# Two of three row blocks of the output projection by seven block products instead of eight, with the order of all operations in a table

## The chip, the cores and the metric

The kernel runs on one core of a Trainium2 chip. The core has a matrix engine (TensorE, PE in the profile, with its weight loads as PEld), a vector engine (VectorE, DVE), a scalar engine (ScalarE, ACT), a general engine (GpSimd, POOL) and a synchronisation engine (SyncE, SP), which here issues most DMA transfers. The metric is the device time of one execution in microseconds (us); less is better. All durations below come from the profile of one execution of the kernel before, the times from separate runs of it.

## What is computed

Attention over blocks of keys, followed by a gated feed-forward network. Cut to what matters:

```python
# q, k, v: 4 batches, 8 heads, 768 positions, 64 per head
ub = sum(maximum(q * k_min[chunk], q * k_max[chunk]))   # bound per query and chunk of 32 keys
sel = the 6 chunks of largest ub that are causal
attn = softmax(where(sel & causal, q @ k.T / 8, -1e9)) @ v
x = attn, heads side by side            # 3072 rows of 512
gate = sigmoid(x @ w_gate)              # 512 -> 1536
val  = x @ w_val                        # 512 -> 1536
out  = (gate * val) @ w_out             # 1536 -> 512, float32
```

The change touches the last line only: the output projection, a product of (3072 x 1536) by (1536 x 512).

## The kernel before, in words

The 24 row blocks of 128 positions (4 batches of 6) are gathered into eight units, u0 to u7, of three row blocks (384 rows) each. For every unit but u0 (which holds three first blocks with an attention of their own, the operations with an f in their names) the work is:

- Preparation: keys and queries are loaded, turned, and put into 16-bit operands (`kT`, `kt`, `hk`, `qf`, `qm`, `hq`); the bounds (`ub`, L1007) and the choice of chunks (`ubn`, `mx`, `ap`, `apt`, `hqm`) follow on DVE. Units u1 and u2 load keys and queries in rows and turn them on PE (`kn`, `kT`, `qn`, `qT`, L906); later units load whole batches (`k_1` to `k_3`, `q_1` to `q_3`) and turn them on DVE.
- Attention (`attend`): scores `sc` on PE (L1068), `exp` on ACT (L1079), the causal mask `cm` on POOL (L1085), the product with v, `pv`, on PE (L1101), the division `rz` and `x` on DVE, and a transpose `xps` on PE (L1128) with its copy `xT`.
- Feed-forward (`ffn`): for each of the 12 blocks of 128 hidden columns, `g` and `v` (each four matmuls of 128x384, L1151), `tanh` on ACT (L1159) and `hg` = (tanh + 1) * v on DVE (L1163). Then for each of the three row blocks (`tb` = 0, 1, 2) the output projection: 12 matmuls of 128x512 in three operations `o0`, `o1`, `o2` of four (L1176), the eviction `osb` with the factor 0.5 on ACT or DVE (L1185, L1186), and the store `out` of 128 rows of 2 KB by SP (L1187). In u7 the last row block goes in two parts, 384 and 128 columns (`o`, `ob`).

The weights `wg`, `wv`, `wo` come in three pieces each by DMA from POOL's queue (L723, L724, L729), converted to 16 bits on the way; POOL issues them between its other operations. The inputs are loaded through SP's queue in its order, the stores too.

The order of the work is set before the program is emitted. The functions above only add operations to a `Plan`, each with the engines that may run it and an estimated cost. `Plan.order` then places them: it walks time forward with those costs, and takes at each step the ready operation with the best priority; the priorities carry small offsets from a table (`NUDGES`), and landing times of DMAs come from another (`LANDS`). So every engine has one fixed list, and runs it in order. Buffers are numbered slots of a few kinds; PSUM is the kind `ps` with eight slots (banks), `big` is two large slots that hold the raw keys and queries of a batch one after the other, `hg` has 18 slots.

The operations that the prediction follows are, by their names before `_u`: `o0`, `o1`, `o2`, `osb`, `out` (these change), `g`, `v`, `hg`, `kT`, `qT`, `kn` (these keep their work and change place), and the DMA issues.

## Time and profile before

| | us |
|---|---|
| device time, median of 3 runs | 295.19 (294.67 to 295.32) |
| span of the profiled execution, first to last instruction | 293.1 |
| PE busy | 278.2 (95%) |
| ACT busy | 195.6 (67%) |
| DVE busy | 188.6 (64%) |
| POOL busy | 91.6 (31%) |
| granted TensorE clock, mean | 0.999 |

The profiled execution's own device time is not listed apart from the three runs. Its span is 293.1 us, and the median of the runs lies 2.1 us above the span; that part is start and end of the execution outside the program's own instructions.

How to read it: PE's busy time is that of its matmuls, whose ends are modelled and which overlap, so the duration of one matmul (379 ns for 128x512) is not what it costs in a row of matmuls. What it costs is the distance from one start to the next, which the chain and the timeline show: a line of either gives a start, a length and a number of instructions.

### The profile page before, as it was taken

How to read it: one execution, taken by the hardware profiler on the slowest of the kernel's cores; microseconds unless marked ns; L12 is line 12 of the kernel's file. 1: busy time of each engine (PE TensorE's matmuls, PEld its weight loads, DVE VectorE, ACT ScalarE, POOL GpSimd, SP SyncE). 2: the span in 40 equal slices, each digit the busy share in tenths (PEclk: the TensorE clock that was granted, in tenths of full speed). 3: DMA queues.
4: the chain of work that ended last, by engine and by line, in shares of the span. 5: the costliest groups of instructions: out<-in, count | busy, mean ns of one | idle time of the engine just before them, and what ended most of it. 6: DMA issues, size and time to landing. Idle time of an engine off the chain costs nothing.

```text
span 293.1 us, 6981 instructions
## 1 busy us (share of the span) xinstructions
PE 278.2 (95%) x2668; PEld 178.3 (61%) x2668; DVE 188.6 (64%) x560; ACT 195.6 (67%) x399; POOL 91.6 (31%) x162
## 2 busy tenths in 40 slices
PE   2849999999999999999999999999999999999995
PEld 2636655767674566556667667676566556655653
DVE  8366874997999289999999989654134114423320
ACT  7655847977984879458899998877463366332421
POOL 6744304834652337013326864212000010000000
PEclk9999999999999999999999999999999999999999
DMA  7999999989934999299992300001100020001002
GB/s 164 201 252 237 197 202 218 231 154 203 176 62 84 217 190 195 49 231 184 198 179 67 118 3 3 0 2 39 72 2 1 36 74 0 2 36 74 0 2 107
DMA packets 123377, 32.69 MB, mean 112 GB/s; under 512 B 111440, under 2 KB 120400, under 8 KB 123344
## 3 DMA queue, kind: packets, MB, share of 16 engines
q1 hardware_dynamic: 118592, 27.53, 44.5%
q0 software_dynamic: 4752, 4.72, 9.7%
q8 instruction: 21, 0.34, 0.5%
q14 instruction: 12, 0.10, 0.1%
HBM read 30.67 MB, written 6.29 MB: 126 GB/s over the span
## 4 chain that ended last, share of the span: by engine, by line
PE 76%; DMA 12%; DVE 6%; POOL 2%; SPq 1%; issue 1%; ACT 0%; DVEq 0%; ACTq 0%
PE o_u L1176 20%; PE v_u L1151 17%; PE g_u L1151 17%; PE sc_u L1068 10%; DMA wo<-in_moe_w_out_dram 8%; PE pv_u L1101 6%; DMA kq_u<-in_k_dram 3%; PE ube_u L1007 2%; PE xps_u L1128 2%; DMA vf<-in_v_dram 1%; SPq L747 1%; DVE kt L958 1%; DVE kx L792 1%; DVE kcr L792 1%; DVE qf_u L974 1%
## 5 line engine op out<-in xcount | busy, mean ns | idle before, releaser
L1079 ACT ACTIVATE att_u<-sc_u 128x512 f16<-128x512 f32 (+3 forms) x184 | 88.1, 551 | 14.4 <-PE sc_u L1068 13.6
L1163 DVE SCALAR_TENSOR_TENSOR hg_u<-gate_u,v_u 128x384 f16<-128x384 f16 x96 | 52.0, 546 | 54.1 <-PE v_u L1151 36.7
L1151 PE MATMUL g_u<-xT_u,wg 128*128 128x384 f16 x384 | 79.2, 329 | 0.0
L1151 PE MATMUL v_u<-xT_u,wv 128*128 128x384 f16 x384 | 78.8, 328 | 0.0
L1159 ACT ACTIVATE gate_u<-g_u 128x384 f16<-128x384 f32 x96 | 47.6, 496 | 38.4 <-DVE hg_u L1163 21.5
L1176 PE MATMUL o_u<-wo,hg_u 128*128 128x512 f16 (+1 forms) x288 | 67.4, 377 | 0.7 <-DMA wo<-in_moe_w_out_dram 0.7
L1085 POOL TENSOR_SCALAR_AFFINE_SELECT att_u<-att_u 128x384 f16<-128x384 f16 (+1 forms) x56 | 28.2, 509 | 109.7 <-ACT att_u L1079 108.9
L1151 PEld LDWEIGHTS <-wv 128*128 128x128 f16 x384 | 36.9, 98 | 22.9 <-issue 0.7
L1151 PEld LDWEIGHTS <-wg 128*128 128x128 f16 x384 | 36.5, 99 | 21.8 <-issue 1.5
L1176 PEld LDWEIGHTS <-hg_u 128*128 128x128 f16 x300 | 27.9, 98 | 27.8 <-issue 1.1
L1185 ACT ACTIVATE osb_u<-o_u 128x512 f32<-128x512 f32 (+1 forms) x20 | 12.0, 598 | 26.3 <-PE o_u L1176 24.6
L1101 PEld LDWEIGHTS <-att_u 128*128 128x128 f16 x640 | 25.5, 98 | 4.7
L1101 PE MATMUL pv_u<-v,att_u 128*128 128x65 f16 x640 | 27.9, 193 | 0.0
L1068 PE MATMUL sc_u<-hqo,hko 128*128 128x128 f16 (+2 forms) x220 | 27.8, 243 | 0.1
L1068 PE MATMUL sc_u<-hqe,hke 128*128 128x128 f16 (+2 forms) x220 | 27.2, 243 | 0.2 <-ACT att_u L1079 0.2
L1068 PEld LDWEIGHTS <-hke 128*128 128x128 f16 x220 | 16.8, 98 | 5.7 <-issue 1.2
L1068 PEld LDWEIGHTS <-hko 128*128 128x128 f16 x220 | 16.3, 98 | 4.8 <-issue 0.2
L784 POOL CAST v<-v 128x512 f16<-128x512 f32 x23 | 13.9, 616 | 13.5 <-DMA v<-in_v_dram 13.3
L581 DVE COPY xT_u<-xps_u 128x384 f16<-128x384 f16 (+1 forms) x17 | 5.8, 338 | 14.4 <-PE xps_u L1128 14.3
L1120 DVE TENSOR_TENSOR x_u<-pv_u,rz_u 128x384 f16<-128x384 f32 (+1 forms) x28 | 14.5, 524 | 0.4
L1030 DVE MAX8 mx_u<-ubn_u 128x8 f32<-128x8 f32 (+16 forms) x152 | 12.4, 158 | 0.1
L792 DVE TRANSPOSE_TENSOR_REDUCE kcr<-k 128x24 f32<-128x768 f32 x12 | 11.3, 945 | 0.0
(121 smaller groups left out, 308.4 us busy)
## 6 DMA issues: line engine op xcount, KB each, us to landing
v<-in_v_dram SPq DMA_DIRECT2D x23, 256.0 KB, 4.7
out_dram<-osb_u SPq DMA_DIRECT2D x23, 256.0 KB, 2.3
k<-in_k_dram SPq DMA_DIRECT2D x12, 384.0 KB, 4.8
q<-in_q_dram SPq DMA_DIRECT2D x12, 384.0 KB, 5.6
wg<-in_moe_w_gate_dram POOLq DMA_DIRECT2D x3, 512.0 KB, 9.0
wv<-in_moe_w_val_dram POOLq DMA_DIRECT2D x3, 512.0 KB, 10.9
wo<-in_moe_w_out_dram POOLq DMA_DIRECT2D x3, 512.0 KB, 21.4
kf<-in_k_dram SPq DMA_DIRECT2D x8, 128.0 KB, 3.1
```

Source lines behind the costliest of these rows:

```text
L784: plan.add(f"v16_{b}_{ib}", {POOL: pool(H * D)}, lambda e: nc.gpsimd.tensor_copy(v16[b % 2][:, ib, :, 0:D], at(t)), reads=[t], writes=[("v ...
L792: plan.add(f"kx{m}_{name}_{p}", {DVE: dve(size)}, lambda e, m=m, op=op: nc.vector.tensor_reduce(out=outs[m](), in_=src(), op=op, axis=AX.X ...
L1030: nc.vector.max(at(mx)[:, e_, j, :], at(ubn)[:, e_, j, 0:max(8, u.seen[j])])
L1068: nc.tensor.matmul(at(t)[:, o:o + 128 * m], hk[b % 2][e_][:, p, 128 * jb:128 * jb + 128], hq[u.side][e_][:, p, 128 * x:128 * (x + m)], sta ...
L1079: plan.add(f"exp_{u.name}_{h}_{y}", {ACT: act(n)}, lambda e, t=t, att=att, b0=b0, n=n: nc.scalar.activation(at(att)[:, b0:b0 + n], at(t), ...
L1085: nc.gpsimd.affine_select(out=dv, in_=dv, compare_op=ALU.is_ge, fill=0.0, base=0, pattern=[[0, u.m], [1, 128]], channel_multiplier=-1)
L1101: nc.tensor.matmul(at(pv)[:, last, x, :], at(att)[:, c:c + 128], v16[b % 2][:, jb, h, :], start=(jb == 0), stop=(jb == ib))
L1120: plan.add(f"x_{u.name}_{p}", {DVE: dve(u.t)}, lambda e: nc.vector.tensor_tensor(at(x_).rearrange("p a (e d) -> p e a d", e=2), at(pv)[:, ...
L1151: nc.tensor.matmul(at(t), w16[:, c, 128 * fb:128 * fb + 128], at(u.xt)[:, c, :], start=(c == 0), stop=(c == 3))
L1159: plan.add(f"tanh_{u.name}_{fb}", {ACT: act(T)}, lambda e, g=g, gate=gate: nc.scalar.activation(at(gate), at(g), AF.Tanh, scale=0.5), read ...
L1163: plan.add(f"hg_{u.name}_{fb}", {DVE: dve(T)}, lambda e, w_=w_, gate=gate, hg=hg: nc.vector.scalar_tensor_tensor(at(hg), at(gate), 1.0, at ...
L1176: nc.tensor.matmul(at(o), at(hgs[fc])[:, 128 * tb:128 * tb + 128], wo16[:, fc, lo:hi], start=(fc == 0), stop=(fc == NFB - 1))
```

## The change

For units u4 to u7, the row blocks 0 and 1 are no longer projected one after the other. The function `pair` treats the two row blocks together as a 2x2 block product: rows in two halves (row block 0, row block 1), the 1536 hidden columns in two halves (of every four column blocks the first two and the last two), and the 512 output columns in two halves of 256. By the scheme of Strassen and Winograd the product of two 2x2 block matrices needs seven block products instead of eight, and sums of blocks before and after:

- `weight_sums` makes four sums of blocks of `w_out` once (`tw0` to `tw3`, in three pieces j each, 12 operations of 128x512 16-bit numbers, DVE or POOL). They live in slot 0 of `big` behind the raw keys of batch 3.
- For each unit, `sw0` to `sw3` (three pieces each, 12 operations of 128x256 16-bit numbers, DVE or POOL) make the sums of hidden blocks. They and the 32-bit results live in slot 1 of `big`, behind the raw queries of batch 3.
- The seven products `p1` to `p7` are each six matmuls of 128x256 in two operations (four and two matmuls, the second with a z), into six PSUM banks; `p2` and `p6` share one.
- Six evictions `p1s`, `c11`, `u4`, `c12`, `c22`, `c21` (`c11` and `c22` are 512 wide, the others 256) add the products up in SBUF; all but `p1s` read SBUF and PSUM on DVE. `c11` takes `p2` and `p6` together.
- Then the two stores of 128 rows of 2 KB.

The third row block of each unit, and units u0 to u3, are projected as before. `hg` becomes nine slots of two column blocks each. The key "ffn", which kept the feed-forward products of all units in the order in which they were added, is gone. The planner (`walk`, `landings`, `settle`, the priorities) is gone too: `Plan.order` reads one table with every operation and its engine, and one with every buffer's slot.

```diff
-    def order(self):
-        nudge = {n: int(x) for n, x in (w.rsplit(":", 1) for w in NUDGES.split())}
...
-        out = self.walk({op: lands[op.name] for op in self.ops if op.dma is not None}, prio=prio)
-        out, _ = self.settle([(op, op.engine) for op in out])
+    def order(self):
+        ops = {op.name: op for op in self.ops}
...
+        for w in ORDER.split():
+            name, _, e = w.partition("=")
+            op = ops[name]
+            op.engine = {"P": PE, "A": ACT, "V": DVE, "G": POOL, "S": SP}[e]
...
+ORDER = """
+kf1_0=S kf0_0=S ident=G kfT_0=P kf16_0=A epat0=V epat=G hkp011=G hkp000=V hkp001=A hkp100=V hkp010=V ap1=V v10=G k2_u1=S kn_u1_2=V
+qf1_0=S kf0_1=S qf0_0=S qfT_0=P kT_u1_2=P kxf1=V ap0=V ident16=V kcr0=V qf16_0=A scf_0=P expf_0_1=A cmf_0_1=G qf1_1=S wg0=G
...
+xpsf_1_0=P expf_1_1=A cmf_1_1=G hkf1=G vf1_2=G wv0=G kx1_u1_0=V kt_u1_0=V expf_2_0=A cmf_2_0=G expf_2_1=A cmf_2_1=G hkf0=G wv1=G
...
+c12_u7=V c22_u7=V out_u7_0=S osbb_u7_2=A o0_u7_2=P o2_u6_2=P osb_u6_2=A out_u6_2=S outb_u7_2=S o1_u7_2=P o2_u7_2=P osb_u7_2=V
+out_u7_2=S p4_u7=P p4z_u7=P c21_u7=V out_u7_1=S
...
+    PAIRED = (4, 5, 6, 7)
+    tw = Buf("big", "tw", [128, 4, 3, 2, 256], F16)
+    sw = Buf("big", "sw", [128, 3072])
...
+            for n, (a, b) in enumerate(((12, 11), (22, 0), (22, 12), (21, 1))):
+                made.append(plan.add(f"tw{n}_{j}", {POOL: pool2(512), DVE: dve(512, 2)}, lambda e, n=n, a=a, b=b, w=w, out_=out_: both(e).tensor_tensor(
+                    out_(n), w[a](), w[b]() if b > 1 else out_(b), ALU.subtract),
...
+        def product(name, to, side, a, b, reads):
+            for part, js in (("", (0, 1)), ("z", (2,))):
+                def emit(e, js=js):
+                    for j in js:
+                        for i in range(2):
+                            nc.tensor.matmul(at(to)[:, side], a(j)[:, i], b(j)[:, i], start=j == i == 0, stop=j == 2 and i == 1)
...
+        product("p1", p1, 0, lambda j: block(j, 0, 0), w_(0, 0), h(0))
...
+        product("p2", p26, 0, lambda j: block(j, 0, 1), w_(1, 0), h(1))
+        product("p6", p26, 1, lambda j: sums(1, j), t_(1), st(1, 1))
+        onto("c11", p26, 2, slice(0, 3, 2), lambda: four()[:, 1:2].to_broadcast([128, 2, 256]), [key[1]])
+        product("p5", p5, 0, lambda j: sums(0, j), t_(0), st(0, 0))
+        onto("u4", p5, 1, slice(3, 4), lambda: four()[:, 2:3], [key[2]])
+        product("p3", p3, 0, lambda j: sums(3, j), w_(1, 1), lambda j: [(sw, j, 3)])
+        onto("c12", p3, 1, slice(1, 2), lambda: four()[:, 3:4], [key[3]])
+        store(u, 0, "", lambda: at(sw)[:, 1536:2048], rows[0], 0, 512, [key[0], key[1]], next_)
+        product("p7", p7, 0, lambda j: sums(2, j), t_(2), st(2, 2))
+        onto("c22", p7, 2, slice(2, 4), lambda: four()[:, 2:4], [key[2], key[3]])
+        product("p4", p4, 0, lambda j: block(j, 1, 1), t_(3), lambda j: h(1)(j) + [(tw, 3, j)])
+        onto("c21", p4, 1, slice(2, 3), lambda: four()[:, 2:3], [key[2]])
+        store(u, 1, "", lambda: at(sw)[:, 2048:2560], rows[1], 0, 512, [key[2], key[3]], next_)
...
-        for tb in range(3):
+        if u.i in PAIRED:
+            pair(u, hgs, [rows[0], rows[1]], next_)
+        for tb in range(2 if u.i in PAIRED else 0, 3):
```

In the table the letter behind a name is its engine (P for PE, A for ACT, V for DVE, G for POOL, S for SP), and each engine runs its entries in the order of the table. What it does differently from the list before, as far as the prediction speaks of it:

- On SP the first loads were `kf0_0 qf0_0 kf1_0 qf1_0 vf_0` and so on, with the eight loads of u1 behind the 15 of the first blocks. Now `kf1_0 kf0_0` come first, `k2_u1` third and `k0_u1` eleventh; `k3_u1` is the 22nd load in both.
- On PE, `kT_u1_3`, `qT_u1_0`, `qT_u1_1` and `qT_u1_2` stood behind `g_u0_0`; now they stand ahead of it. The scores of u1 stand ahead of `g_u0_8` to `g_u0_11`.
- On POOL, two operations lay between `wg0` and `wv0`; now eight lie between (`v16_0_0 cmf_0_0 cmf_1_0 vf1_1 vc_1 cmf_1_1 hkf1 vf1_2`, then `wv0`), and `wv1` comes ahead of `wg1`. The sums `tw` and `sw` go to POOL in 6 and 26 cases and to DVE in 6 and 22.
- Of the operations that both have, 40 move from DVE to ACT, 24 from ACT to DVE, 27 from ACT to POOL, 23 from DVE to POOL, 11 from POOL to ACT and 6 from POOL to DVE.
- At the end, PE's last entries were `o` and `ob` of the third row block of u7; now they are `o1_u7_2 o2_u7_2 p4_u7 p4z_u7`, with `osb_u7_2` and `c21_u7` on DVE and the stores `out_u7_2` and `out_u7_1`.

721 lines of the change are left out of this document (304 added, 417 removed), and 2 rows, old and new, of the table plan.

## The prediction, made before the result was known

> **What bounds the kernel now.** I read the page's busy times first, then busy time by stage, then PE's waits, then the chain.
>
> ```profile
> PE 278.2 (95%) x2668; PEld 178.3 (61%) x2668; DVE 188.6 (64%) x560; ACT 195.6 (67%) x399; POOL 91.6 (31%) x162
> ```
>
> ```profile
> core 0: us, PE busy (x) PEld busy (x) DVE busy (x) ACT busy (x) POOL busy (x), PEclk, DMA share, GB/s
> 0.00:23.20 23.20, 13.05 (x94) 9.87 (x95) 14.02 (x38) 15.09 (x25) 14.22 (x29) 1.00 0.98 212
> 23.20:50.00 26.80, 25.89 (x182) 14.99 (x181) 17.97 (x61) 17.63 (x41) 7.99 (x15) 1.00 1.18 210
> 50.00:90.00 40.00, 39.33 (x480) 27.38 (x477) 36.49 (x100) 34.74 (x78) 23.20 (x44) 1.00 0.91 169
> 90.00:290.00 200.00, 199.94 (x1924) 126.05 (x1916) 120.10 (x364) 127.87 (x259) 46.21 (x76) 1.00 0.35 76
> 290.00:293.10 3.10, 0.00 (x0) 0.00 (x0) 0.00 (x0) 0.26 (x1) 0.00 (x0) 0.94 0.24 85
> ```
>
> The stages carry the argument. From 90 to 290 us PE is busy for 199.94 of 200 us, while DVE, ACT and POOL are busy for 120, 128 and 46. In this stage lies all the work of units u4 to u7, so work taken off PE there shortens the kernel one for one, as long as its inputs still come in time. PE's idle time is 10.15 us before 23.2, 0.91 up to 50, 0.67 up to 90, and the 3.1 at the end.
>
> ```profile
> PE kfT L820 <- DMA kf<-in_k_dram: 5.7, 2, 5.0
> PE kT_u L906 <- ACT kn_u L579: 2.4, 1, 2.4
> ...
> PE o_u L1176 <- DMA wo<-in_moe_w_out_dram: 0.7, 1, 0.7
> ```
>
> PE's waits say the same: the first loads, then one wait of 2.4 us for u1's keys, and one of 0.7 us for the last piece of `wo`. Columns: total us, times, longest.
>
> **Term 1, the products.** In a row of matmuls a matmul costs the distance to the next start. The chain gives it for 512 columns, the timeline for 256:
>
> ```profile
> 91.21 5.18 PE o_u L1176 x24
> ```
>
> ```profile
> 143.21 0.38 PE L1068 MATMUL sc_u<-hqo,hko 128*128 128x256 f16 x2
> 143.43 0.38 PE L1068 MATMUL sc_u<-hqe,hke 128*128 128x256 f16 x2
> 143.65 0.65 PE L1151 MATMUL g_u<-xT_u,wg 128*128 128x384 f16 x3
> ```
>
> 24 matmuls of 512 in 5.18 us are 216 ns each, and they are exactly two row blocks. Four of 256 from 143.21 to 143.65 are 109 to 110 ns each (I take 109), each with a weight load of its own, as the new ones have. A unit now spends 24 x 216 = 5.18 us, and will spend 7 x 6 x 109 = 4.58 us. Four units: 4 x 0.606 = 2.42 us less. All of it is on PE's path: **-2.42**.
>
> Could 256 columns be too short to cover the weight load?
>
> ```profile
> L1176 PEld LDWEIGHTS <-hg_u 128*128 128x128 f16 x300 | 27.9, 98 | 27.8 <-issue 1.1
> ```
>
> A load lasts 98 ns, below 109, and the four rows of scores ran at 109 with loads between. The Trainium skill, page "TensorE: Matmul & The Clock Gate", section "Back-to-back issue gap", speaks against the change: it says that in a stream of pairs of load and matmul the spacing is set by both, about 81 ns at 128 columns and 131 at 512. An estimate from these two, 98 ns at 256, would make a unit dearer by 42 x 98 - 24 x 131 = 0.97 us, 3.9 us in all. The trace does not agree with its figure for 512: 216 ns, not 131. I go by the rows.
>
> **Term 2, the sums.** Per unit there are 12 `sw`, two of 512 and three of 256 columns among the results on DVE, and `p1s`; two `osb` go. Once there are 12 `tw`. Prices by the nearest rows:
>
> ```profile
> L1085 POOL TENSOR_SCALAR_AFFINE_SELECT att_u<-att_u 128x384 f16<-128x384 f16 x48 | 24.9, 526 | 100.9 <-ACT att_u L1079 100.3 <-PE sc_u L1068 0.3
> L784 POOL CAST v<-v 128x512 f16<-128x512 f32 x23 | 13.9, 616 | 13.5 <-DMA v<-in_v_dram 13.3
> ...
> L583 POOL COPY hqo<-apt_u 64x768 f16<-64x768 f16 x3 | 2.7, 892 | 5.5 <-DVE apt_u L1041 4.7 <-DVE rz_u L1118 0.8
> ...
> L799 POOL TENSOR_TENSOR kcr<-kx,kcr 128x96 f32<-128x96 f32 x2 | 0.8, 386 | 0.8 <-DVE rz_u L1118 0.8
> ...
> L799 POOL TENSOR_TENSOR kcr<-kx_u,kcr 128x48 f32<-128x48 f32 x1 | 0.3, 285 | 0.1
> ```
>
> ```profile
> L879 DVE TENSOR_TENSOR xf<-pvf,rzf 128x256 f16<-128x256 f32 x8 | 3.3, 420 | 0.1
> ...
> L1186 DVE TENSOR_SCALAR osb_u<-o_u 128x512 f32<-128x512 f32 x4 | 2.7, 676 | 4.2 <-PE o_u L1176 4.2
> ```
>
> On DVE a sum of 256 is at most 0.42 us, a result of 512 is 0.68, so the 22 + 6 sums and 20 results cost some 22 x 0.42 + 6 x 0.68 + 8 x 0.68 + 12 x 0.42 = 24 us of DVE, in a stretch of 200 us in which it now idles for 80. On POOL 48 more elements cost 0.10 us, 2.1 ns each, so 256 cost 0.72 us and 512 cost 1.26: 26 x 0.72 + 6 x 1.26 = 26 us, in a stretch in which it idles for 154. Neither becomes the bound. What can show is the queue behind one product. In u4, POOL must run between the last `hg` that `sw0_u4_1` reads and PE's `p6_u4`, by the table, `sw0_u4_0 tw1_1 sw1_u4_0`, a copy of 768, a cast, a mask, `tw1_2 sw0_u4_1 sw1_u4_1`: 2 x 1.26 + 4 x 0.72 + 0.89 + 0.62 + 0.53, some 7.4 us, while PE's entries from `v_u4_6` to `p6_u4` come to 9.5 us at the distances above. The second half, `p6z_u4`, is 0.4 us later and needs two more sums, 1.44 us, so its margin is about 1 us. Behind a late `p6` stands everything on PE. I take **+0.2** for such waits; ends 0 (the margins hold) and +1.5 (see rival C).
>
> **Term 3, the end.** PE's last work was 12 matmuls of 128 columns, then a copy and a 64 KB store.
>
> ```profile
> L1185 ACT ACTIVATE osb_u<-ob_u x1: 278/278/278, 290.0 to 290.0; 128x128 f32<-128x128 f32 x1
> ```
>
> ```profile
> out_dram<-osb_u SPq DMA_DIRECT2D x23, 256.0 KB, 2.3
> ...
> out_dram<-osb_u SPq DMA_DIRECT2D x1, 64.0 KB, 1.7
> ```
>
> Now `p4z_u7` is last, then `c21` on DVE (0.42 by the row of 256 above, for 0.28) and a store of 256 KB right behind one of 192 KB. That is 0.14 longer for the sum and 0 to 0.6 for the store; I take **+0.45**, ends +0.1 and +0.75. The other stores and sums of u7 lie under the 3.4 us of `o0_u7_2`, `o2_u6_2`, `o1_u7_2`, `o2_u7_2` and `p4` that PE has after `p7z`.
>
> **Term 4, the new order ahead of u4.** This is the unknown; it can be as large as term 1.
>
> ```profile
> 15.63 0.41 PE L886 MATMUL xpsf<-ident,xf 128*128 128x128 f16 x2
> 18.44 0.90 PE L906 MATMUL kT_u<-ident,kn_u 128*128 128x128 f32 x3 [2.40 <-ACT kn_u L579]
> ...
> 23.20 1.49 PE L1151 MATMUL g_u<-xT_u,wg 128*128 128x384 f16 x4
> 24.48 1.49 PE L1151 MATMUL v_u<-xT_u,wv 128*128 128x384 f16 x4
> ```
>
> ```profile
> 15.12 0.92 SPq L758 DMA_DIRECT2D kq_u<-in_k_dram  x1
> ```
>
> ```profile
> kq_u<-in_k_dram SPq DMA_DIRECT2D x4, 192.0 KB, 9.3
> ```
>
> `g_u0_0` starts at 23.20, and the first matmuls cost 0.32 us each (1.28 us for four), twice the 0.163 of later ones: PE comes out of its gaps slow, which costs about 10 x 0.16 = 1.6 us. In the new order `kT_u1_3` stands ahead of `g_u0_0`. Its load, `k3_u1`, is the 22nd on SP as before; it was issued at 15.12, and with 9.3 us to land (the median of the four) is there at 24.4. With 0.5 for its copy and 0.7 for its turn, `g_u0_0` starts at 25.6: 2.4 later, of which four transposes done earlier give back 4 x 0.33 = 1.3. So +1.1, unless PE is at full speed by then, since it turns u1's keys and queries without long gaps just before; that gives up to 1.6 back, -0.5. For the other side, the first product waits for two loads instead of three, and `k2_u1` and `k0_u1` come early enough to fill the gap of 2.4 us after 15.63: gains of up to 3 us if the whole opening moves up with them. From 50 to 90 us, where DVE is busy for 36.5 of 40 us, 63 entries leave DVE and 30 come to it: 0.67 us of PE's waits could go. I take **-0.3** for all of this, near the middle of the walk's -0.5 and +1.1 and a small gain behind it; ends -3 and +1.7.
>
> **The sum.** Span 293.1 - 2.42 + 0.2 + 0.45 - 0.3 = 291.03. The median of the runs lies 2.1 us above the span of the profiled execution, which I carry over: **293.1 us**, 0.7% below 295.19. Ends of the unknown terms around the forecast: 291.0 to 294.6.
>
> **The rivals.**
>
> B. The opening gains what the ends allow: term 4 at -3 gives 290.4. For it speaks that 10.15 us of PE's idle time lie before 23.2; against it that about 4 of these are the first landing, and that the late loads are the same bytes.
>
> C. The sums on POOL come late, in u4 and u5 (20 of the 26 `sw` there). The mechanism is seen in the opening: copies of one shape take longer when POOL and DVE run together.
>
> ```profile
> 4.13 1.51 DVE L581 COPY hko<-epat 64x1536 f16<-64x1536 f16 x3
> ...
> 5.66 1.91 DVE L581 COPY hke<-epat 64x1536 f16<-64x1536 f16 x3
> ...
> 7.10 0.93 POOL L583 COPY hke<-kf 64x512 f16<-64x512 f16 x1
> ```
>
> ```profile
> L583 POOL COPY hqo<-apt_u 64x512 f16<-64x512 f16 x1 | 0.6, 602 | 2.6 <-DVE apt_u L1041 2.6
> ```
>
> The second three DVE copies overlap POOL's copy at 7.10, and take 0.4 us longer; the POOL copy takes 0.93 against 0.60. The Trainium skill's page "SBUF — State Buffer", section "Who interferes with whom", has the rule: DVE and GpSimd share one port pair as a lock, also when a DVE instruction has two SBUF inputs, as the sums have. The rows agree with it. If each of some eight sums in front of a product slips by 0.35 us, that is 2.8 us against margins of 1 to 2: about 1 us in each of u4 and u5, 295.0 us.
>
> D. It ends slower: the weights come late. `wv0` stood two POOL operations behind `wg0`; now eight lie between, the last of which wait for `cmf_1_1` and so for the second block's exponentials.
>
> ```profile
> 9.96 0.93 POOL L723 DMA_DIRECT2D wg<-in_moe_w_gate_dram  x1
> ...
> 12.07 0.76 POOL L724 DMA_DIRECT2D wv<-in_moe_w_val_dram  x1
> ```
>
> ```profile
> wg<-in_moe_w_gate_dram POOLq DMA_DIRECT2D x3, 512.0 KB, 9.0
> ```
>
> ```profile
> 24.56 24.20 DMA wo<-in_moe_w_out_dram
> ```
>
> With the median of 9.0 us `wg0` was there at 19.0. If `wv0` is issued only then, POOL's DMA queue runs dry, and all seven pieces behind it slip by what it loses; the last piece of `wo` landed at 48.76 (24.56 + 24.20), and PE had to wait for it. At that time PE had done 28 us of work at the distances above, so it had lost 20.8; in the new order 33 us of work lie ahead of `o2_u0_0`, and PE comes to it at some 53. A slip below 4 us is covered; one of 7.5 us costs 3.3 us and gives 296.4. It decides from a slip of 6.9 us, where the time is 0.2% above before.
>
> E. The weight loads are not covered at 256 columns: 4 x 18 more loads of 98 ns, 7.1 us, 300 us. The rows at 143.21 speak against it.
>
> **How the numbers follow.** A difference of 0.2% (0.6 us) is about what a measurement of this kernel can tell from none. Forecast 0.53 (291.0 to 294.6, all faster); B 0.17 (faster); C 0.10 (0.08 within 0.2%, 0.02 just faster); D 0.18 and E 0.02 (slower). So faster 0.72, same 0.08, slower 0.20. The range reaches from just below B to D: 290.2 to 296.4.
>
> **What would show it.** Term 1: between starts, 109 ns in the `p` products, 42 of them per unit, and PE still busy for all but 0.3 us from 90 us on. Term 2: PE's waits name no POOL or DVE sum for more than 0.3 us in total, C is right if they do. Term 3: from PE's end to the end of the span 3.6 us, for 3.1. Term 4: the start of the first `g_u`, and PE's idle time before 50 us, 11.1 us now; D is right if PE waits for `wo` or `wv` there. The prediction is wrong above all if term 4 lies outside its ends.

## The result, and the profile after

The changed kernel takes 292.12 us (median of 4 runs, 291.77 to 292.85) against 294.93 us (median of 4 runs, 294.09 to 295.32): a ratio of 0.9913, 95% interval 0.9886 to 0.9939. It is faster, by 2.8 us. The profiled execution took 292.16 us and has a span of 290.5 us, 2.7 us less than before (290.46 for 293.12 in the traces).

The page's busy times of the changed kernel, then its busy time by stage (columns as before; the first stage ends at the start of the first `g_u`):

```profile
PE 275.3 (95%) x2740; PEld 185.4 (64%) x2740; DVE 201.3 (69%) x577; ACT 189.3 (65%) x393; POOL 145.6 (50%) x227
```

```profile
0.00:24.76 24.76, 15.15 (x106) 12.04 (x107) 14.68 (x34) 16.02 (x28) 16.70 (x31) 0.88 0.98 218
24.76:50.00 25.24, 25.19 (x239) 16.18 (x238) 16.35 (x58) 21.47 (x48) 14.46 (x26) 0.98 1.21 211
50.00:90.00 40.00, 40.00 (x433) 26.42 (x432) 35.35 (x104) 31.21 (x69) 25.92 (x46) 1.00 0.99 185
90.00:290.00 200.00, 194.93 (x1968) 130.73 (x1966) 134.89 (x383) 120.56 (x251) 88.49 (x126) 1.00 0.33 73
```

The number ahead of the DMA share is the granted TensorE clock. Here it is 0.50 from 19.0 to 24.76 us. The 1.00 in before's first rows can't be set against it: before's trace has no clock record ahead of 26.5 us, and its first products start 0.32 us apart too.

PE ends at 286.80 instead of 289.94, so 3.2 of the 5.07 us that the last stage is idle lie behind PE's end. PE's waits name two that before didn't have, on DVE's `x_u` and on POOL's mask:

```profile
PE sc_u L891 <- DVE x_u L943: 0.9, 1, 0.9
...
PE pv_u L924 <- POOL att_u L908: 0.8, 1, 0.8
```

**The products** run at the distance that the prediction took. In the timeline of PE, 12 matmuls start at 207.95 and the next at 209.26:

```profile
207.95 1.47 PE L1012 MATMUL p_u<-tw,sw 128*128 128x256 f16 x12
209.26 0.82 PE L1012 MATMUL p_u<-wo,sw 128*128 128x256 f16 x6
```

That is 1.31 us for 12, 109 ns each. No wait of PE names a sum of a product.

**A measure for the rest.** PE's busy time hides short waits, since the modelled ends of matmuls overlap the next start. So I counted for each matmul the distance that it costs in a row (0.417 ns a column and 2.6 ns, which gives 109 at 256 columns and 216 at 512; the 32-bit ones, 360 of 2668 before, by the median of their own distances), and took the sum of the matmuls begun before a time from that time. The difference is what PE has lost until then. All kernels of this section and the next, in us:

| lost until | 25 | 50 | 100 | 160 | 190 | 205 | PE's end |
|---|---|---|---|---|---|---|---|
| before | 14.7 | 18.0 | 20.5 | 23.1 | 25.7 | 25.7 | 25.9 |
| changed | 14.0 | 15.9 | 16.8 | 20.0 | 24.8 | 24.9 | 25.1 |
| products_only | 14.9 | 18.6 | 21.2 | 23.7 | 28.9 | 29.7 | 32.2 |
| products_spread | 13.6 | 18.0 | 20.5 | 23.1 | 25.7 | 29.5 | 30.2 |
| products_u5_u7 | 13.9 | 18.1 | 20.7 | 23.2 | 25.8 | 25.8 | 26.2 |
| order_only | 13.6 | 16.4 | 17.6 | 21.0 | 24.8 | 25.8 | 27.2 |
| order_only2 | 13.2 | 15.7 | 17.2 | 20.3 | 24.1 | 24.6 | 29.1 |
| before_opening | 13.8 | 28.3 | 30.8 | 35.2 | 38.9 | 40.1 | 40.6 |
| new_first35 | 14.1 | 22.4 | 25.4 | 28.0 | 30.6 | 30.6 | 30.8 |
| new_first90 | 14.0 | 16.2 | 18.9 | 21.5 | 24.0 | 24.1 | 24.3 |
| sums_later | 13.2 | 14.8 | 16.3 | 19.6 | 23.5 | 23.5 | 23.8 |
| mask_earlier | 13.9 | 16.2 | 17.6 | 20.7 | 25.5 | 25.6 | 25.9 |
| end_as_before | 13.0 | 14.5 | 15.6 | 18.8 | 23.7 | 23.8 | 24.3 |
| all_three | 14.0 | 16.0 | 17.7 | 20.8 | 24.5 | 24.7 | 25.2 |

PE's work by the same count is 264.03 us before and 261.66 with four paired units. The levels of the table are too high by a part that all rows share. The 288 small 32-bit products of the bounds (`ub`) run eight at a time: seven starts are 7 ns apart, and the next eight follow after 0.06 to 0.3 us. Their median of 7 ns counts most of their time as lost, some 6 us by the end, and about 1.9 us of what each kernel loses between 160 and 190 us. Differences between rows hardly suffer from it.

One kernel's opening differs from execution to execution: the changed kernel and its four relatives at the bottom run the same program there, and have lost 14.5 to 16.2 at 50 us. So a difference between two rows at one time means something from about 2 us, or where it arises inside one stretch. At 100 us these five have lost 15.6 to 17.7, and the four kernels with the order of before 20.5 to 21.2.

The first two rows hold the result. The new order is 3.7 us ahead at 100 us and 3.1 at 160; then it loses 4.8 up to 190 where before loses 2.6, and arrives 0.8 ahead. With 2.37 less work and an end that is 0.5 longer: -0.8 - 2.37 + 0.5 = -2.7, which is the difference of the spans.

**The two new waits.** The first, at 170 us. PE has two `pv_u` done and goes on 1.02 us later, where two take 0.06; POOL, whose mask it needs, ran an operation of 2.12 us (`qm_u7_0`, moved to POOL by the table; its sister took 0.85 on ACT) and, in its order, another mask and a copy ahead of that mask. Timeline of PE, then of POOL, then of ACT:

```profile
170.46 0.22 PE L924 MATMUL pv_u<-v,att_u 128*128 128x65 f16 x2
171.48 0.47 PE L924 MATMUL pv_u<-v,att_u 128*128 128x65 f16 x10 [0.79 <-POOL att_u L908]
```

```profile
167.34 2.12 POOL L631 TENSOR_SCALAR qm_u<-qf_u 128x768 f32<-128x768 f32 x1 [1.78 <-PE ubo_u L830]
169.43 0.52 POOL L908 TENSOR_SCALAR_AFFINE_SELECT att_u<-att_u 128x384 f16<-128x384 f16 x1
170.01 0.82 POOL L406 COPY hko<-kt 64x768 f16<-64x768 f16 x1
170.90 0.52 POOL L908 TENSOR_SCALAR_AFFINE_SELECT att_u<-att_u 128x384 f16<-128x384 f16 x1
```

```profile
167.17 0.85 ACT L629 ACTIVATE qm_u<-qf_u 128x768 f32<-128x768 f32 x1 [0.93 <-PE ubo_u L830]
```

The second, at 182 us. PE waits for the division `x_u6_1`; by the count above this costs 1.10 us. In front of the division DVE has three sums of the weights, which take 1.03, 0.76 and 0.82 us where others of the same shape take 0.41. Timeline of PE, of DVE, and of POOL beside it:

```profile
183.63 0.38 PE L891 MATMUL sc_u<-hqe,hke 128*128 128x128 f16 x4 [0.94 <-DVE x_u L943]
```

```profile
179.16 1.03 DVE L976 TENSOR_TENSOR tw<-wo 128x512 f16<-128x512 f16 x1
180.12 0.54 DVE L1086 SCALAR_TENSOR_TENSOR hg_u<-gate_u,v_u 128x384 f16<-128x384 f16 x1
180.59 0.76 DVE L976 TENSOR_TENSOR tw<-wo 128x512 f16<-128x512 f16 x1
181.26 0.82 DVE L976 TENSOR_TENSOR tw<-wo,tw 128x512 f16<-128x512 f16 x1
...
183.04 0.53 DVE L943 TENSOR_TENSOR x_u<-pv_u,rz_u 128x384 f16<-128x384 f32 x1
...
193.37 0.41 DVE L976 TENSOR_TENSOR tw<-wo 128x512 f16<-128x512 f16 x1
```

```profile
178.88 1.04 POOL L406 CAST hqe<-qf_u 64x768 f16<-64x768 f32 x1
180.55 0.52 POOL L908 TENSOR_SCALAR_AFFINE_SELECT att_u<-att_u 128x384 f16<-128x384 f16 x1 [0.63 <-ACT att_u L902]
181.01 0.80 POOL L607 CAST v<-v 128x512 f16<-128x512 f32 x1
...
193.44 0.72 POOL L908 TENSOR_SCALAR_AFFINE_SELECT att_u<-att_u 128x384 f16<-128x384 f16 x1
```

POOL's three operations end at 179.92, 181.07 and 181.81; the three sums end at 180.19, 181.35 and 182.08, each 0.27 to 0.28 us behind. Each sum began while POOL was at work and finished at a fixed distance from POOL's end. It goes the other way round as well: the sum at 193.37 began 0.07 us ahead of a mask of POOL and took its 0.41, and that mask took 0.72 us for the usual 0.52.

**The end.** `p4` is the last product, then `c21` and its store:

```profile
285.98 0.82 PE L1012 MATMUL p_u<-tw,hg_u 128*128 128x256 f16 x6
...
286.83 0.42 DVE L1029 SCALAR_TENSOR_TENSOR sw<-p_u,sw 128x256 f32<-128x256 f32 x1
287.28 0.33 SPq L1053 DMA_DIRECT2D out_dram<-sw  x1
```

From PE's end to the end of the span it is 3.66 us, for 3.18 before.

### The profile page after: what moved, and what is told of

Its sections match the earlier page's. It is cut to its first block, busy times and chain, and to the rows that moved or that the text cites. A ratio compares the mean times of both kernels' runs of the same rounds, so it can differ in the third digit from the quotient of the medians.

```text
span 290.5 us, 7177 instructions
## 1 busy us (share of the span) xinstructions
PE 275.3 (95%) x2740; PEld 185.4 (64%) x2740; DVE 201.3 (69%) x577; ACT 189.3 (65%) x393; POOL 145.6 (50%) x227
## 4 chain that ended last, share of the span: by engine, by line
PE 90%; POOL 3%; DVE 2%; issue 1%; DMA 1%; SPq 1%; ACT 0%; POOLq 0%; ACTq 0%
PE g_u L1073 21%; PE v_u L1073 21%; PE o_u L1101 14%; PE sc_u L891 11%; PE p_u L1012 6%; PE pv_u L924 6%; PE ube_u L830 2%; PE xps_u L951 1%; PE kT_u L729 1%; DMA qf<-in_q_dram 1%; PE qT_u L729 1%; PE qfT L643 1%; PE kfT L643 1%; DVE tw L976 1%; SPq L570 1%
## 5 line engine op out<-in xcount | busy, mean ns | idle before, releaser
L1086 DVE SCALAR_TENSOR_TENSOR hg_u<-gate_u,v_u 128x384 f16<-128x384 f16 x96 | 51.2, 544 | 50.0 <-PE v_u L1073 25.1
L1073 PE MATMUL g_u<-xT_u,wg 128*128 128x384 f16 x384 | 74.2, 327 | 0.0
L1073 PE MATMUL v_u<-xT_u,wv 128*128 128x384 f16 x384 | 72.5, 326 | 0.0
L908 POOL TENSOR_SCALAR_AFFINE_SELECT att_u<-att_u 128x384 f16<-128x384 f16 (+1 forms) x56 | 28.3, 513 | 38.0 <-ACT att_u L902 36.8
L1101 PE MATMUL o_u<-wo,hg_u 128*128 128x512 f16 (+1 forms) x192 | 45.2, 376 | 0.0
L1101 PEld LDWEIGHTS <-hg_u 128*128 128x128 f16 x204 | 19.2, 98 | 18.3 <-DMA wo<-in_moe_w_out_dram 0.4
L891 PE MATMUL sc_u<-hqo,hko 128*128 128x128 f16 (+2 forms) x220 | 25.9, 243 | 0.0
L891 PE MATMUL sc_u<-hqe,hke 128*128 128x128 f16 (+2 forms) x220 | 24.4, 243 | 1.1 <-DVE x_u L943 0.9
L891 PEld LDWEIGHTS <-hko 128*128 128x128 f16 x220 | 16.3, 98 | 3.8 <-issue 0.4
L998 POOL TENSOR_TENSOR sw<-hg_u 128x256 f16<-128x256 f16 x7 | 4.7, 668 | 25.8 <-DVE hg_u L1086 25.8
L607 POOL CAST v<-v 128x512 f16<-128x512 f32 x23 | 14.5, 639 | 3.7 <-issue 2.2
L998 POOL TENSOR_TENSOR sw<-hg_u,hg_u 128x256 f16<-128x256 f16 x6 | 4.0, 667 | 23.2 <-DVE hg_u L1086 23.2
L943 DVE TENSOR_TENSOR x_u<-pv_u,rz_u 128x384 f16<-128x384 f32 (+1 forms) x28 | 14.8, 529 | 0.6
L631 POOL TENSOR_SCALAR qm_u<-qf_u 128x768 f32<-128x768 f32 (+3 forms) x6 | 10.0, 1674 | 8.7 <-DVE qf_u L797 6.7
L1029 DVE SCALAR_TENSOR_TENSOR sw<-p_u,sw 128x256 f32<-128x256 f32 (+1 forms) x20 | 10.6, 528 | 3.2 <-PE p_u L1012 2.7
```

Source lines behind the costliest of these rows:

```text
L607: plan.add(f"v16_{b}_{ib}", {POOL: pool(H * D)}, lambda e: nc.gpsimd.tensor_copy(v16[b % 2][:, ib, :, 0:D], at(t)), reads=[t], writes=[("v ...
L891: nc.tensor.matmul(at(t)[:, o:o + 128 * m], hk[b % 2][e_][:, p, 128 * jb:128 * jb + 128], hq[u.side][e_][:, p, 128 * x:128 * (x + m)], sta ...
L908: nc.gpsimd.affine_select(out=dv, in_=dv, compare_op=ALU.is_ge, fill=0.0, base=0, pattern=[[0, u.m], [1, 128]], channel_multiplier=-1)
L943: plan.add(f"x_{u.name}_{p}", {DVE: dve(u.t)}, lambda e: nc.vector.tensor_tensor(at(x_).rearrange("p a (e d) -> p e a d", e=2), at(pv)[:, ...
L1029: plan.add(f"{name}_{u.name}", {DVE: dve(256 * n)}, lambda e: nc.vector.scalar_tensor_tensor(four()[:, lo], at(src) if n == 1 else at(src) ...
L1073: nc.tensor.matmul(at(t), w16[:, c, 128 * fb:128 * fb + 128], at(u.xt)[:, c, :], start=(c == 0), stop=(c == 3))
```

## The experiments

Theory, from the profile: the products bring their 2.4 us; the new order brings more ahead of 100 us than was predicted; and two waits at 170 and 182 us, one of them caused by sums, take part of it back. The first rival: the sums cost what the products save, and all of the gain is the order. The second: the order is worth only what was predicted.

### The products alone, in the order before

**products_only.** The list of before; at the places of `o0`, `o1`, `o2` of row blocks 0 and 1 stand the products. For each of the units u4 to u7, and with one sum of the weights behind each of u4's blocks:

```diff
-hg_u4_3=V
+hg_u4_3=V tw3_0=V sw0_u4_0=V sw1_u4_0=V sw3_u4_0=V
...
-o0_u4_0=P
+p1_u4=P
-o1_u4_0=P
+p1z_u4=P p1s_u4=A p2_u4=P
-o2_u4_0=P
+p2z_u4=P p6_u4=P p6z_u4=P c11_u4=V
-o0_u4_1=P
+p5_u4=P p5z_u4=P u4_u4=V
```

> The order of all operations as in the kernel before; only the seven products, their sums and their evictions stand in place of the projections of row blocks 0 and 1 of u4 to u7; every sum is made by DVE, right behind the hidden block it reads, and the end is that of before. Theory T (the products are worth 2.42 us as counted; what the new order gains ahead of u4 is larger than predicted, some 3.4 us, and two new waits of 1 us each between 165 and 185 us eat part of it): this kernel has the first part alone, so 2.4 us below before, less a few tenths for late sums: 0.992 of before, 292.3 to 293.0 us, with 42 matmuls at 109 ns between starts per unit. Rival R (the sums cost what the products save, and the new order makes the whole gain): 294.5 to 295.5, ratio 1.000, with waits of PE on the sums of 2 us or more. Prices: DVE some 0.29 us for a sum of 256 and 0.415 for one of 512 where POOL is idle.

Measured: 298.18 us, ratio 1.0118 (1.0100 to 1.0136). It is slower, which neither side had. PE's work went down by 2.37 us as in the changed kernel, but behind 160 us it lost 8.4 us where before loses 2.8. The largest of its waits that grew against before (total us, times, longest; before it has 0.3, 1, 0.3):

```profile
PE xps_u L960 <- DVE x_u L952: 2.2, 3, 1.6
```

This is again a wait for divisions; ahead of the longest one DVE has four sums in a row. The reason that I take for it is in the kernel before, in a table by 4 us that the prediction did not ask for; the next two runs test it:

```profile
180.00:184.00 4.00, 4.00 (x52) 2.95 (x48) 3.97 (x20) 3.44 (x9) 2.20 (x3) 1.00 0.02 6
...
204.00:208.00 4.00, 4.00 (x25) 2.03 (x23) 0.83 (x3) 2.33 (x6) 1.01 (x2) 1.00 0.17 66
```

DVE (third of the busy times) is full at 180 us and has little to do from 204 on. The 80 us in which it idles are not where u4's sums have to be made.

**products_spread.** The same with the weights' sums on POOL and u4's sums behind 191 us:

```diff
-hg_u4_0=V tw0_0=V
+hg_u4_0=V
...
-cm_u6_4=G
+cm_u6_4=G tw1_0=G tw2_0=G
...
-hg_u4_8=V
+hg_u4_8=V sw2_u4_0=V sw0_u4_0=V sw1_u4_0=V sw3_u4_0=V
```

> As products_only (order of before, seven products in place of the two row blocks), but the sums are made elsewhere: the twelve sums of the weights on POOL between 184 and 205 us, the sums of u4's hidden blocks on DVE behind its ninth block, where DVE is busy for less than half of the time, those of the other units one block later, the first product's copy on DVE. In products_only PE was held 5.6 us longer than before behind 175 us, at divisions, copies and sums that stood in DVE's list behind the new sums. Theory T2 (the products are worth their 2.4 us and what they lost was the place of the sums): 292.4 to 293.6, ratio 0.992 to 0.996. Rival R2 (the products need the new order ahead of them, since in the order of before PE waits for the sums wherever they stand): above 295, ratio over 1.002, with 3 us or more of waits on POOL's or DVE's sums or on the masks behind them.

Measured: 296.27 us, ratio 1.0040 (1.0021 to 1.0059). At 50, 100, 160 and 190 us PE has lost what it had lost before, to 0.1 us; from 190 to 205 it loses 3.8 us more. Timeline of DVE, then of POOL in the same microseconds:

```profile
191.58 1.15 DVE L1008 TENSOR_TENSOR sw<-hg_u 128x256 f16<-128x256 f16 x1
192.65 1.24 DVE L1008 TENSOR_TENSOR sw<-hg_u,hg_u 128x256 f16<-128x256 f16 x1
193.92 0.29 DVE L1008 TENSOR_TENSOR sw<-sw,hg_u 128x256 f16<-128x256 f16 x1
...
195.15 0.54 DVE L1096 SCALAR_TENSOR_TENSOR hg_u<-gate_u,v_u 128x384 f16<-128x384 f16 x1
195.61 1.09 DVE L1008 TENSOR_TENSOR sw<-hg_u 128x256 f16<-128x256 f16 x1
```

```profile
191.42 1.15 POOL L986 TENSOR_TENSOR tw<-wo 128x512 f16<-128x512 f16 x1
192.53 1.21 POOL L986 TENSOR_TENSOR tw<-wo,tw 128x512 f16<-128x512 f16 x1
...
195.40 1.15 POOL L986 TENSOR_TENSOR tw<-wo 128x512 f16<-128x512 f16 x1
```

POOL's sums end at 192.57, 193.74 and 196.55, and DVE's at 192.73, 193.89 and 196.70: 0.15 or 0.16 us later each time, whenever they began. The sum at 193.92, with POOL idle, takes 0.29. The hidden block at 195.15, which reads one source from PSUM, takes its 0.54 with POOL at work. So a DVE instruction with both sources in SBUF that begins beside a running POOL instruction stands still until that one is over. The Trainium skill's page "SBUF — State Buffer", section "Who interferes with whom", states such a rule: two SBUF inputs contend with a GpSimd instruction that reads SBUF, at most one does not (outside modes that use both port pairs), and the shared port pair is an exclusive lock. These rows agree with it. Rival R2 had waits of this size, but its reason was another; whether the products need the new order was left open by this run.

**products_u5_u7.** The same list, but u4 projected as before, all sums on DVE, the weights' sums among u5's hidden blocks:

```diff
-PAIRED = (4, 5, 6, 7)
+PAIRED = (5, 6, 7)
...
-cm_u6_4=G tw1_0=G tw2_0=G
+cm_u6_4=G
...
-hg_u5_0=V
+hg_u5_0=V tw0_0=V tw1_0=V
```

> Order of before; the seven products in u5, u6 and u7 only, u4 projected as before; every sum on DVE, the twelve of the weights spread over u5's feed-forward, where DVE was busy for some 1.5 of 4 us and POOL for next to nothing; no sum on POOL. In products_spread a DVE sum of 256 took 0.29 us alone and 1.1 to 1.2 us where a sum of POOL ran beside it, and PE lost 4.3 us between 190 and 205 us to divisions and copies behind them; from 205 us on it lost only 0.5 us. Theory T3 (the products are worth 0.606 us a unit in the old order too; what eats it is DVE's and POOL's shared time in u4's stretch): 3 x 0.606 = 1.8 us, less 0.2 to 0.6 for late evictions: ratio 0.994 to 0.996, and no DVE sum above 0.5 us. Rival R2 (the products need the new order): 1.000 or above.

Measured: 293.12 us, ratio 0.9944 (0.9923 to 0.9964), 1.5 us below before's median of the same session. PE lost 0.3 us more than before, its work is 1.78 less. No wait names a sum, and none of the weights' sums is stretched:

```profile
L984 DVE TENSOR_TENSOR tw<-wo x6: 418/418/419, 212.0 to 224.1; 128x512 f16<-128x512 f16 x6
```

(Minimum, median and maximum in ns.) So the products bring 0.5 to 0.6 us a unit in the old order as well (1.5 us of time, 1.78 of work, in three units), and rival R2 is out. What they need, by these rows, is room on DVE with POOL quiet beside it. The run left out u4, took the sums off POOL and made them later, all at once; which of the three is enough was not tried apart.

### The new order alone

**order_only.** The changed kernel's list, without products and sums; row blocks 0 and 1 by 12 matmuls of 512 columns each at places of the products:

```diff
-p1_u4=P p1z_u4=P p1s_u4=V
+o0_u4_0=P o1_u4_0=P
...
-p2_u4=P p2z_u4=P
+o2_u4_0=P
```

> The order and engines of the changed kernel for every operation that both have, but row blocks 0 and 1 of u4 to u7 are projected by 12 matmuls of 512 columns each, at the places of the products, and there are no sums. Theory T: the products' 2.42 us come back, and the wait of 1.1 us at 182 us goes, because the three sums of the weights ahead of it on DVE are gone; the wait of 0.96 us at 170 us stays, because it hangs on a moved operation of POOL and not on a sum: 1.3 us above the changed kernel, 1.5 below before, ratio 0.995, PE's wait on DVE for a division gone. The prediction's own terms (order -0.3, end +0.45): 295.1, ratio 1.0005. Rival R (order alone makes the gain): as the changed kernel, 0.991.

Measured: 296.10 us, ratio 1.0035 (1.0019 to 1.0051). By that number the prediction's own terms were nearest, but the trace shows another reason. Up to 190 us this kernel has lost 24.8, as the changed one: the mask's wait at 170 us is there, the wait for the division at 182 is not, as theory T said, and the loss between 160 and 190 is 3.7 for 4.8. Behind 190 us it loses 2.4 us, the changed kernel 0.3:

```profile
PE o_u L990 <- ACT att_u L902: 1.3, 2, 0.8
```

Two of the eight projections wait, 1.3 us together, for banks that ACT has yet to read. **order_only2** gave them other places, each row block in one piece:

```diff
-o0_u4_0=P o1_u4_0=P
...
-o2_u4_0=P
+o0_u4_0=P o1_u4_0=P o2_u4_0=P osb_u4_0=A
```

> As order_only (new order, no products, no sums), but with other places and banks for the eight projections: in order_only PE waited 0.93 and 0.69 us at 204 and 209 us for a bank that held scores of which ACT had yet to take the exponential, which the changed kernel doesn't do. Theory T: without these, and with the opening as in the changed kernel, 1.3 us above it, 293.4, ratio 0.9955. The prediction's terms: 295.1, ratio 1.0005. If the new order is worth nothing without the products: as order_only, 1.0035.

Measured: 298.93 us, ratio 1.0116 (1.0085 to 1.0147). It missed too: until 190 us it has lost 24.1, less than both kernels, and then 5.0 us more, among them 0.7, 0.5 and 1.2 us for exponentials and for copies of transposes. The new order behind 190 us is arranged round products of 0.65 us; that pieces of 2.6 us in it put scores late would explain the waits, but was not shown. These two runs settle what the two waits hang on, and nothing about the worth of the order as a whole.

**new_first90.** Before, without products or sums, with the first 615 operations of the new list (to u1's output projection, some 88 us), then the old list:

```diff
-kcr0=V ident=G kf0_0=S epat0=V qf0_0=S v10=G
...
+kf1_0=S kf0_0=S ident=G kfT_0=P kf16_0=A epat0=V
...
 o0_u1_0=P
```

> The same with the first 615 operations of the new order (up to u1's output projection, some 88 us), then the order of before. Theory T: 3.5 us gained by 97 us and kept to the end, since the rest has the waits of before: 291.2 to 292, ratio 0.989. If the gain only pulls PE into waits that come later (both kernels lose some 5 us between 100 and 190 us): 293 to 294.5, ratio 0.995 to 0.999. The prediction's term 4 (-0.3): 294.4, 0.999.

Measured: 293.14 us, ratio 0.9915 (0.9888 to 0.9941): without a single product it is as fast as the changed kernel. At 90 us its trace has lost 17.4 us, for 20.4 before; it gives back 1.4 up to 100, in two waits at the seam, and ends 1.65 us ahead. Between theory T (0.989) and the middle case (0.995), nearer to T; the prediction's -0.3 is excluded.

**new_first35.** Only the first 199 operations, some 33 us, then the old list:

```diff
-kcr0=V ident=G kf0_0=S epat0=V qf0_0=S v10=G
...
+kf1_0=S kf0_0=S ident=G kfT_0=P kf16_0=A epat0=V
...
 g_u0_6=P
```

> The kernel before, without products or sums, but with the first 199 operations of the new order (up to the tenth product of u0's feed-forward, some 33 us), then the order of before. Theory T: PE reaches u0's feed-forward with 1.1 to 1.5 us less lost and keeps it: 293.3 to 293.7, ratio 0.995 to 0.996. The prediction's walk (the first product of u0 later by 1 to 2 us, half of it given back): 294.7 to 295.8, ratio 1.000 to 1.004. Lost in the middle (what comes next is bound by loads, not by PE): 294.4 to 295.0, 1.000.

Measured: 298.40 us, ratio 1.0104 (1.0042 to 1.0166). Slower, outside all three cases. PE's timeline has a wait of 1.17 us for a hidden block of DVE at 38.57, and then:

```profile
41.25 1.14 PE L1074 MATMUL g_u<-xT_u,wg 128*128 128x384 f16 x3 [1.87 <-DMA wg<-in_moe_w_gate_dram]
...
42.50 1.49 PE L1074 MATMUL v_u<-xT_u,wv 128*128 128x384 f16 x4
43.78 1.49 PE L1074 MATMUL g_u<-xT_u,wg 128*128 128x384 f16 x4
```

```profile
43.00:47.00 4.00, 4.00 (x15) 1.83 (x13) 0.34 (x1) 0.73 (x2) 0.00 (x0) 0.50 1.24 211
```

From 40.2 to 47.0 us the granted clock is 0.50 (in the row, the number ahead of the DMA share): the 20 matmuls from 41.25 take 6.1 us, 0.32 between starts, for 3.3 us at the 0.163 of the full clock. So the slow clock costs 2.8 us, more than the wait for `wg`, which PE's idle time alone would not show.

The new POOL list issues the weights later (the first piece of `wv` at 19.0 us, for 12.1). With the old PE order behind it, PE comes to the last piece of `wg` at some 39 us and stands until 41.25. The changed kernel comes to it at 41.24 without a wait, because u1's scores are ahead of `g_u0_8`:

```profile
37.29 2.00 PE L891 MATMUL sc_u<-hqe,hke 128*128 128x256 f16 x23
...
41.24 2.11 PE L1073 MATMUL g_u<-xT_u,wg 128*128 128x384 f16 x12
```

**before_opening.** The other way round: the first 196 operations as before, then the new list.

```diff
-kf1_0=S kf0_0=S ident=G kfT_0=P kf16_0=A epat0=V
...
+kcr0=V ident=G kf0_0=S epat0=V qf0_0=S v10=G
...
 g_u0_6=P
```

> The changed kernel, but the first 196 operations of the list (all up to the seventh product of u0's feed-forward, some 33 us) in the order, on the engines and in the buffers of before; the rest in the new order. By the starts of PE's operations the new order stands 1.5 us ahead of before at 33 us and 3.5 us ahead at 97 us. Theory T (gains of both stretches, independent of each other): 1.5 us above the changed kernel, 293.6, ratio 0.996. If the opening only shifts waits that come later anyway: within 0.4 us of the changed kernel, 0.991. If the opening makes all of the order's gain: 3.4 us above it, 295.5, ratio 1.002. PE's first product of u0 at 23.2 us with its first four matmuls at 0.32 us each, as before.

Measured: 307.36 us, ratio 1.0428 (1.0410 to 1.0446), outside all three cases. In the new list POOL casts a piece of v ahead of the copies that u1's scores need; in the old list of loads that piece comes late, and POOL's queue stands for 15 us:

```profile
48.78 0.61 POOL L616 CAST v<-v 128x512 f16<-128x512 f32 x1 [14.89 <-DMA v<-in_v_dram]
```

That is a fault of the seam, and the run says nothing about the gain of the opening. Together the three runs show no gain of the first 35 us by themselves. The order of the loads, POOL's list and the scores ahead of `g_u0_8` hang together, and by the table the gain arises between 25 and 100 us.

### The two waits and the end

**sums_later.** The three sums of the weights behind the division, in front of `tw3_0`:

```diff
-ap1_u7=V tw0_0=V hg_u4_0=V
+ap1_u7=V hg_u4_0=V
...
-tw2_0=V tw1_0=V rz_u6_1=V mx0_u7=V x_u6_1=V
+rz_u6_1=V mx0_u7=V x_u6_1=V
...
-tw3_0=V
+tw0_0=V tw2_0=V tw1_0=V tw3_0=V
```

> The changed kernel, with three sums of the weights (tw0_0, tw2_0, tw1_0) moved on DVE from in front of a division of u6 to behind five hidden blocks' worth of later work, in front of tw3_0. Theory T (these three took 1.04, 0.76 and 0.82 us because POOL ran casts and a mask at the same time, and the division that PE waits for stood behind them): PE's wait of 1.1 us at 182 us goes and nothing takes its place, 1.0 us below the changed kernel, ratio 0.988; where POOL is idle at their new place the sums take 0.415 us each. Rival (PE is ahead of its inputs there and waits for the next thing anyway): within 0.3 us of the changed kernel, ratio 0.991, a wait of the same size on another operation within 10 us.

Measured: 291.30 us, ratio 0.9887 (0.9868 to 0.9906). The wait is gone, and the loss between 160 and 190 us falls from 4.84 to 3.90. The sums at their new place:

```profile
186.18 0.75 DVE L985 TENSOR_TENSOR tw<-wo 128x512 f16<-128x512 f16 x2
186.85 0.88 DVE L985 TENSOR_TENSOR tw<-wo,tw 128x512 f16<-128x512 f16 x2
```

Four of them (`tw3_0` is the fourth) take 1.55 us together, with POOL idle from 186.02 to 187.79. That is theory T by the trace; by the times alone it is no proof, since this interval and the changed kernel's (0.9886 to 0.9939) overlap.

**mask_earlier.** `qm_u7_0` behind the mask:

```diff
-qm_u7_0=G
...
-cm_u5_4=G
+cm_u5_4=G qm_u7_0=G
```

> The changed kernel with one operation of POOL (qm_u7_0, which took 2.12 us) moved behind the mask cm_u5_4 that PE waits for. Theory T: PE's wait of 0.96 us at 170 us on POOL's mask goes, the products of queries and bounds that need qm_u7_0 come 0.7 us or more after it is done, so nothing takes its place: 0.9 us below the changed kernel, ratio 0.988 to 0.989. Rival (PE then waits for qm_u7_0 itself, or for the next mask): within 0.3 us of it, 0.991, with a wait of PE on POOL's or ACT's qm near 172 us.

Measured: 292.84 us, ratio 0.9927 (0.9904 to 0.9951), no gain over the changed kernel. The mask's wait went, and another of the same size came four microseconds later. POOL, then PE:

```profile
169.95 0.52 POOL L917 TENSOR_SCALAR_AFFINE_SELECT att_u<-att_u 128x384 f16<-128x384 f16 x1 [1.51 <-ACT att_u L911]
170.44 2.13 POOL L640 TENSOR_SCALAR qm_u<-qf_u 128x768 f32<-128x768 f32 x1
```

```profile
175.54 0.55 PE L900 MATMUL sc_u<-hqe,hke 128*128 128x256 f16 x6 [1.05 <-POOL hqe L415]
```

POOL now idles 1.51 us ahead of the mask and does the 2.13 us later, with a cast, a copy, a mask and then the copy that PE needs behind it. In the changed kernel POOL is busy for 3.87, 3.82 and 3.80 of each 4 us from 168 to 180 us, and this change of order inside its queue only moved the wait. To take the operation to another engine was not tried.

**end_as_before.** `p4_u7`, `c21_u7` and their store ahead of the last row block, the 12 matmuls of 128 columns last:

```diff
-p7z_u7=P
+p7z_u7=P p4_u7=P p4z_u7=P
...
-p4_u7=P p4z_u7=P c21_u7=V out_u7_1=S
+o0b_u7_2=P o1b_u7_2=P o2b_u7_2=P osbb_u7_2=A outb_u7_2=S
```

> The changed kernel with the end of before: the seventh product p4_u7, its sum c21_u7 and its store ahead of the last row block, and PE's last work the 12 matmuls of 128 columns. Prediction's term 3 (the end is 0.1 to 0.75 longer): from PE's end to the end of the span 3.1 us again for 3.7, 0.6 us below the changed kernel, ratio 0.989. Rival (the stores queue up all the same, and the end is set by the last store of 256 KB): 3.5 us or more, within 0.2 us.

Measured: 291.65 us, ratio 0.9905 (0.9873 to 0.9938). From PE's end to the end of the span it is 3.20 us, nearly the 3.18 of before. The median is 0.5 us below the changed kernel's; against its interval that is no proof, but the stretch itself is measured in the trace.

**all_three.** The three edits together.

> The changed kernel with all three: the three sums of the weights later on DVE, POOL's qm_u7_0 behind the mask, the end as before. If the three are independent, 1.0 + 0.9 + 0.6 = 2.5 us below the changed kernel by the trace, 289.6 to 290.2, ratio 0.982 to 0.984, and PE's waits behind 100 us all below 0.3 us. If a gain early only pulls PE into the next late input, 290.5 to 291.3, 0.985 to 0.988.

Measured: 290.60 us, ratio 0.9866 (0.9836 to 0.9896), the lowest time of all, 4.0 us below before and 1.5 below the changed kernel. It is the second case of the expectation: the wait behind the mask stays (1.0 us on `hqe`), and the other two gains add. In its trace the loss between 160 and 190 us is 3.7 for 4.8, and the end takes 3.21 us for 3.66; the profiled execution is the slowest of its six and had lost 0.9 us more in the opening, so its total loss, 25.2, is not below the changed kernel's.

## Why the prediction was right, and where it was not

The forecast was 293.1 us; 292.12 is inside its own range, by the forecast and not by a rival. Step by step, for the span: predicted -2.42 + 0.2 + 0.45 - 0.3 = -2.07; measured -2.37 + 1.10 + 0.48 - 1.87 = -2.66. Two terms were right. Two were off, by +0.9 and by -1.6 us, and more than half of that cancelled, which is luck. The range 291.0 to 294.6 is not what the terms' own ends give, either: -3 and +1.7 in term 4 alone reach from 290.4 to 295.1.

- **What bounds the kernel.** That work taken off PE behind 90 us shortens the kernel nearly one for one is confirmed (products_u5_u7: 1.78 us less work, 1.5 us less time). That DVE idles for 80 us of that stage is true as a sum and misled: the mean of 200 us joined a stretch in which DVE has no idle time with one in which it has little to do. products_only shows the price, 5.6 us.
- **Term 1**, the products: 109 ns, 2.37 us. The weight loads are covered; rival E is out. The estimate from the Trainium skill's figures (page "TensorE: Matmul & The Clock Gate", section "Back-to-back issue gap"), 98 ns for 256 columns against 131 for 512, has no support here: the trace has 109 and 216.
- **Term 2**, the waits for sums: mis-sized, +1.10 for +0.2, within its ends. The prediction looked at POOL's queue in front of `p6_u4` and gave it a margin of 1 us; that held, and no product waits. What it did not do was to list what stands in DVE's queue behind the six sums of the weights: a division that PE needs. The sums on POOL were dearer in the forecast (0.72 and 1.26) than in the trace:

```profile
L998 POOL TENSOR_TENSOR sw<-hg_u,hg_u 128x256 f16<-128x256 f16 x6 | 4.0, 667 | 23.2 <-DVE hg_u L1086 23.2
```

```profile
L976 POOL TENSOR_TENSOR tw<-wo,tw 128x512 f16<-128x512 f16 x4 | 4.6, 1152 | 2.6 <-DVE tw L976 2.6
```

- **Term 3**, the end: +0.48 for +0.45, and end_as_before takes it away.
- **Term 4**, the new order: mis-sized, -1.87 for -0.3 (-0.77 lost in all, less the 1.10 of term 2). Up to 100 us it was -3.7, beyond its end of -3; the stretch behind gave 1.8 back, 1.0 of it by POOL's mask at 170 us. The step that failed was to price the opening by the walk to the first `g_u` (25.6 predicted, 24.76 measured) and the rest by PE's idle time, 0.91 and 0.67 us. The kernel before lost 3.3 us from 25 to 50 and 2.6 from 50 to 100, and PE's idle time shows about a quarter of each. If the products of the bounds are counted as the groups of eight that they are and the 32-bit turns at 109 ns, it lost 2.6 and 2.4, and idle time shows a third and a quarter. The first products of u0 ran slow in both kernels, for a shorter time after the change: eight matmuls in 1.76 us, 24.76 to 26.52, for 2.55 before. The granted clock is back at 1.00 from 25.7 us in the changed kernel's trace, and from 26.5 in before's.

```profile
24.76 1.92 PE L1073 MATMUL g_u<-xT_u,wg 128*128 128x384 f16 x8
26.52 0.49 PE L729 MATMUL qT_u<-ident,qn_u 128*128 128x128 f32 x3
```

- **Around the span** 2.1 us were carried over, from the median of three runs and the span of another execution; the changed kernel's execution has 292.16 - 290.5 = 1.7. That is 0.4 of the 1.0 us by which the forecast lies above the result.
- **Rival B** had the size of the gain up to 100 us, by another road: it argued from the idle time ahead of 23.2 us, where little changed (14.7 and 14.0 lost at 25 us), and it did not see that the gain would be partly lost again. **Rival C** named the right mechanism, DVE and POOL in each other's way, and the wrong victim: here it is DVE that stands still, the sums of the weights that grow, by 0.35 to 0.62 us each, and a division that is late. Of POOL's 26 `sw`, 25 took 666 to 672 ns. **Rival D**: the weights are issued late as it said. In new_first35, where nothing covers that, PE waits 1.87 us for them and then runs 2.8 us longer at the halved clock, a cost that the rival's price did not hold; the whole run is 3.2 us slower than before, another wait included. The cover it allowed for, more work ahead on PE, holds in the changed kernel.

What stays open: which of the moved operations between 25 and 100 us brings how much, where the other 0.8 us that the new order gives back between 100 and 190 us go, and what the order behind 190 us is worth without the products. Alone, the products in three units brought 1.5 us and the new order up to 88 us 2.0; the changed kernel has 2.8, and all_three, without the wait at 182 us and the longer end, 4.0.

## What to carry to other kernels

Fewer matmuls in a stage where PE is the bound are worth their distances, if the work that replaces them finds an engine idle at that time: look at a helper engine's load in windows of a few microseconds, not over the stage, and list what stands behind each added operation in its queue. Work with two SBUF sources on DVE should not run beside POOL. A wait of PE can cost more than its length, if the granted clock falls behind it. And compare two orders by the time that PE has lost against the distances of its matmuls: in the kernel before, idle time showed a quarter to a third of what PE lost between 25 and 100 us. A group of matmuls that run side by side must be counted as one.
